# A recurrence and MLP kernel: A of odd chunks stored with exchanged blocks, two K/B buffers, earlier V and r loads

## The chip, the cores and the metric

The kernel runs on one core of one Trainium2 chip. The metric is the device time of one execution in microseconds. A profile is one execution taken by the hardware profiler.

## The reference

For each of 4 batches and 8 heads a 40 x 40 state runs over 768 tokens; its outputs, heads side by side, go through a token-mixing and a channel-mixing MLP:

```
for t in range(S):                                   # S = 768
    y[t]  = r[t] @ state
    Sa    = state @ a[t]
    state = state * w[t][None, :] - outer(Sa, b[t]) + outer(v[t], k[t])
u   = x + (relu(x.T @ w_tok1) @ w_tok2).T            # x: 768 x 320, w_tok1: 768 x 256
out = u + relu(u @ w_ch1) @ w_ch2                    # w_ch1: 320 x 1536
```

All inputs are fp32 (the MLP weights arrive as wide numbers and are split into pairs that TensorE multiplies).

## The kernel before

**Chunks.** Tokens are cut into chunks of 64, 48 in all, numbered g over the batches, 12 per batch. Inside a chunk the recurrence is solved in closed form: a product of A with K and B (px), a triangular 64 x 64 inverse per head, and products with it (ph). From chunk to chunk only the state is handed on (pq, pS, pU); y comes two chunks at a time into the bank yb.

**Preparation** (`t_prep`, one batch in four quarters of 16 tokens): loads w, a, k, b (`pin`, 96 partitions = head x chunk), scans the decays, scales, and stores K/B, A and the decays to the DRAM tiles `sKB`, `sA`, `sP`.

**Pairs** (`t_ab`, `t_a`): two chunks share the buffer `KBp`, loaded from `sKB`, and one of six `AT` buffers, loaded from `sA`. TensorE transposes them (pk, pa) and multiplies (px); the 32 x 32 diagonal blocks go into `Dg`, the blocks off the diagonal into `N21`.

**Solve** (`t_solve`): for a set of eight chunks at once VectorE transposes `Dg` (L748), inverts all 32 x 32 blocks row by row (L770, L772) and transposes the result (L826, L831). In the first two sets it inverts 16 x 16 blocks, and `merge` completes them with TensorE products pm (L927), in four 32 x 32 places of the array.

**Joining the blocks** (`t_b`, per pair): the 64-inverse is made of two 32-inverses T1, T2 and the block T1 N21 T2. With the heads of a chunk in two halves of the partitions, pe = N21 T is computed (L976), copied by ScalarE (`ET`, L984), multiplied again, pt (L1005), and copied into `TBD` (L1011) beside the copies of the diagonal blocks (L968 to L970). ph (L1029) uses `TBD` and `AT`.

**V and r** (`t_load`, `t_v`): v and r of a chunk go into one of three buffers `W2s`, K/B of the chunk into `KB`; pv transposes them (L271, the helper for all transposes).

**MLP** (`t_mlp`): lines L1502 and L1612, the weights of which (`t_piece`: conversion in pieces cv_t, cv_c, stores to sT, sG) are loaded by GpSimd's queue.

**What sets the order.** All work stands in generators; `Planner` runs them in a model of the chip and issues every instruction where its model first finds its engine free, by rank (the numbers of the table `K`). So the order on each engine is fixed when the kernel is built: engines and the SP queue, which issues nearly all DMAs, work in that order and wait by semaphores. When the model sees TensorE idle it puts in a filler (L372), a bf16 product whose result isn't used.

Of the kernel before, what the change touches and what calls it, by code (L numbers as in the profile page):

```python
# [24 lines left out]

K = dict(lat=[200.0, 150.0, 145.0, 90.0], aff=0.92, sets=[8, 8, 8, 8, 8, 8], atn=6, kbp=1, ld=6.75, v=0.89, vg="PA",
         tbd_early=39.4, tbd=[["PD", "AD", "PD", "A"], ["PD", "PD", "A", "P"]], alt_c=1, slack=-10000.0, evm=9.95,
         slack_c=560.87, p_rc=[0, 0, 0, 2], p_a=[0, 2, 0, 1], p_k=[2, 2, 2, 1], solve=[5.59, 4.52, 4.55, 6.79, 6.26,
         -5.24], solve_span=4.19, atomic=0, a=10.07, a_span=3.08, b=2.06, chain=-0.25, evac=0.43, y=-0.77, utr=5.3,
         pem=2, mrg=3.17, ea=9.74, prp=12, psp=12, w=3, c=2, m=2, warm=37, fill=19, fill_cols=4661, prep=[-15.76,  # L30
         -9.38, 9.96, 18.64], prep_step=[2.75, 1.08, 1.04, 1.23], mlp=[11.72, 24.75, 34.32, 41.84], mlp_span=[15.13,
         11.98, 12.78, 11.38], conv_t=6.5, conv_t_span=-10.1, conv_c=3.53, conv_c_span=11.08, conv_after=1)

# [212 lines left out]
def tile_kernel(ctx, tc, r, k, v, w, a, b, wt1, wt2, wc1, wc2, out, dbg=None):  # L246
# [152 lines left out]
    def t_prep(bi):  # L399
# [9 lines left out]
        for q in range(NQ):  # L409
# [18 lines left out]
            def comp(q=q, d=d, ring=ring, tsl=tsl):  # L428
# [518 lines left out]
    def t_b(g):  # L947
# [24 lines left out]

        def pe(z, p, h):
            def f():
                q0, q1 = h * 64, h * 64 + 32
                nc.tensor.matmul(d["pe"][q0:q0 + L, z * NP + p, :], lhsT=o[z]["n21"][q1:q1 + L, p, :],  # L976
                                 rhs=TBt[q1:q1 + L, :, (ci + z) * NP + p], start=True, stop=True)
            return ("PE", (57, 35, "D"), f)

        def etc(h):  # L980
            def f():
                if h == 0:
                    d["et"] = ph.tile([128, 2 * NP, L], F32, tag="ET", name=f"ET{g}", bufs=1)
                nc.scalar.copy(out=d["et"][h * 64:h * 64 + L], in_=d["pe"][h * 64:h * 64 + L])  # L984
            return ("ACT", 372, f)
# [13 lines left out]
        now = yield [etc(0), etc(1)]
        P.rel(tk, now)  # L1000

        def pt(z, p, h):
            def f():
                q0 = h * 64
                nc.tensor.matmul(d["pt"][q0:q0 + L, z * NP + p, :], lhsT=TBn[q0:q0 + L, :, (ci + z) * NP + p],  # L1005
                                 rhs=d["et"][q0:q0 + L, z * NP + p, :], start=True, stop=True)
            return ("PE", (57, 35, "D"), f)

        def tin(h):
            q0 = h * 64  # L1010
            return ("ACT", 372, lambda: nc.scalar.copy(out=TBDb[q0:q0 + L, :, L:2 * L], in_=d["pt"][q0:q0 + L]))  # L1011
        d["pt"], tk = yield from bank("w", [128, 2 * NP, L], f"pt{g}")
        now = yield [pt(*x) for x in zph]
# [808 lines left out]
```

## Time and profile before

| | |
|---|---|
| median of 3 runs | 954.62 us (947.91 to 956.86) |
| the profiled execution | 954.88 us, span 953.2 us |
| TensorE busy | 843.6 us (89%), mean granted clock 0.916 |
| VectorE, ScalarE, GpSimd busy | 607.1 (64%), 531.0 (56%), 227.0 us (24%) |
| DMA | 145.83 MB, mean 153 GB/s |

The span runs from the first to the last instruction; the time adds what lies around it. Matmuls are pipelined, so a busy TensorE is not one at its peak. A wait is put down to what ended it.

### The profile page before, as it was taken

The numbers are of one execution on the slowest core, as the hardware profiler recorded it, in microseconds if no ns is written. First come the engines' busy times: TensorE is split into PE (matmuls) and PEld (weight loads), VectorE is DVE, ScalarE is ACT, GpSimd is POOL, SyncE is SP. The second block draws the span as 40 slices with busy tenths as digits, with TensorE's granted clock in tenths as the row PEclk, the third lists the DMA queues.
The fourth block names the chain that finished last, engine by engine and source line by source line (L and its number), as shares of the span: only waits on it lengthen the run. The fifth ranks groups of instructions, "written<-read, shape, count | busy, mean of one in ns | idle before, by whom it ended". The sixth has DMA issues, their size and how long they took to land.

```text
span 953.2 us, 34564 instructions
## 1 busy us (share of the span) xinstructions
PE 843.6 (89%) x14605; PEld 758.2 (80%) x14605; DVE 607.1 (64%) x1538; ACT 531.0 (56%) x1412; POOL 227.0 (24%) x304
## 2 busy tenths in 40 slices
PE   2666778998898878899998999999989999999997
PEld 2655667887787767788887887999878899998997
DVE  7656885688548978349974498535984544454443
ACT  4266645876659766566675754566535454443221
POOL 5213474343335424021422011001211111001000
PEclk7788886997779869989999998999999999999999
DMA  6698866588585793929458665535356534345522
GB/s 189 177 210 212 202 181 177 144 214 184 154 205 141 180 271 89 233 41 231 132 115 201 147 182 130 110 74 138 82 153 177 127 100 90 74 133 155 183 91 86
DMA packets 244720, 145.83 MB, mean 153 GB/s; under 512 B 205520, under 2 KB 222672, under 8 KB 241488
## 3 DMA queue, kind: packets, MB, share of 16 engines
q1 hardware_dynamic: 238224, 96.37, 44.6%
q0 software_dynamic: 6336, 47.19, 15.4%
q8 instruction: 117, 1.92, 0.9%
q14 instruction: 43, 0.35, 0.1%
HBM read 109.12 MB, written 34.41 MB: 151 GB/s over the span
## 4 chain that ended last, share of the span: by engine, by line
PE 59%; DMA 14%; DVE 12%; issue 6%; ACT 6%; SPq 3%; POOL 0%; DVEq 0%; ACTq 0%; POOLq 0%
PE m L1502 15%; PE m L1612 13%; DMA W2s<-in_r_dram 4%; PE pm L927 3%; SPq L388 3%; PE pq L1095 2%; PE pq L1120 2%; PE pt L1005 2%; PE pv L271 2%; PE ph L1029 2%; DMA cv_t<-in_moe_w_tok_dram 2%; PE yb L372 2%; PE px L670 2%; PE pq L1115 2%; PE pe L976 2%
## 5 line engine op out<-in xcount | busy, mean ns | idle before, releaser
L1612 PE MATMUL m<-ut,wg_c 128*128 128x256 f32 x1152 | 175.5, 294 | 0.2
L1612 PEld LDWEIGHTS m<-ut,wg_c 128*128 128x128 f32 x1152 | 150.0, 191 | 6.6 <-issue 0.9
L1502 PE MATMUL m<-wg_c,hd 128*128 128x320 f32 x864 | 153.6, 321 | 1.3 <-DVE hd L1624 1.1
L1502 PEld LDWEIGHTS m<-wg_c,hd 128*128 128x128 f32 x864 | 130.0, 191 | 5.9 <-DVE hd L1624 1.5
L1622 ACT ACTIVATE hd<-m 128x256 fp32r<-128x256 f32 x144 | 55.3, 384 | 121.3 <-PE m L1612 119.8
L1624 DVE SCALAR_TENSOR_TENSOR hd<-m,hd 128x256 fp32r<-128x256 f32 x144 | 60.8, 422 | 77.3 <-ACT hd L1622 76.4
L1652 DVE TENSOR_TENSOR x<-m,x 128x320 f32<-128x320 f32 x96 | 46.9, 489 | 63.8 <-PE m L1502 63.4
L372 PE MATMUL yb<-ident 128*128 128x192 bf16 x693 | 80.7, 274 | 3.8 <-DVE P L1267 2.0
L385 POOL TENSOR_TENSOR cv_c<-cv_c 128x320 f32<-128x320 f32 (+3 forms) x54 | 58.3, 1086 | 97.8 <-ACT cv_c L1338 70.7
L372 PEld LDWEIGHTS <-ident 128*128 128x128 bf16 x693 | 66.1, 109 | 10.0 <-issue 4.0
L707 ACT ACTIVATE Dg<-px 128x128 f32<-128x128 f32 x144 | 56.1, 390 | 14.0 <-PE px L670 9.7
L1437 POOL DMA_DIRECT2D wg_c<-sG x32 | 17.6, 551 | 149.0 <-PE m L1612 73.7
L271 PE MATMUL pv<-ident,W2s 128*104 128x128 f32 x192 | 32.9, 289 | 19.5 <-DMA W2s<-in_r_dram 16.9
L970 POOL COPY TBD<-TBt 32x256 f32<-32x256 f32 x33 | 22.2, 673 | 111.2 <-PE ph L1029 85.8
L1235 PE MATMUL yb<-KB,RM 128*64 128x40 f32 x768 | 48.0, 230 | 0.0
L385 POOL TENSOR_TENSOR pin<-pin,RC 96x640 f32<-96x640 f32 x19 | 33.8, 1787 | 59.4 <-DVE RC L493 38.1
L1237 PE MATMUL yb<-VSs,RBs 104*64 104x40 f32 x768 | 47.6, 229 | 0.0
L1209 ACT COPY VSs<-pU 40x160 f32<-40x160 f32 x88 | 25.1, 285 | 38.1 <-PE pU L271 36.6
L271 PE MATMUL pk<-ident,KBp 128*104 128x128 f32 x192 | 35.2, 301 | 12.3 <-DMA KBp<-sKB 12.3
L1129 POOL TENSOR_TENSOR RM<-G,upp 64x128 f32<-64x128 f32 x30 | 16.4, 554 | 119.4 <-ACT G L1110 119.1
L641 ACT COPY KBT<-pk 104x512 f32<-104x512 f32 x48 | 27.9, 586 | 26.7 <-PE pk L271 26.1
L1235 PEld LDWEIGHTS yb<-KB,RM 128*64 128x64 f32 x768 | 40.8, 137 | 1.7 <-issue 0.8
(202 smaller groups left out, 1961.8 us busy)
## 6 DMA issues: line engine op xcount, KB each, us to landing
wg_c<-sG POOLq DMA_DIRECT2D x16, 1152.0 KB, 5.9
wg_c<-sG POOLq DMA_DIRECT2D x16, 960.0 KB, 5.5
wg_t<-sT POOLq DMA_DIRECT2D x8, 1280.0 KB, 7.2
sKB<-pin SPq DMA_DIRECT2D x16, 480.0 KB
KBp<-sKB SPq DMA_DIRECT2D x48, 160.0 KB
KB<-sKB SPq DMA_DIRECT2D x48, 160.0 KB
sG<-cv_c SPq DMA_DIRECT2D x24, 192.0 KB
pin<-in_w_dram SPq DMA_DIRECT2D x16, 240.0 KB
```

What stands on the lines that cost most here:

```text
L271: nc.tensor.matmul(out_, lhsT=in_, rhs=idn, start=True, stop=True, is_transpose=True)
L372: nc.tensor.matmul(yb[:, 320:512], lhsT=zf[:, 0:128], rhs=zf[:, 0:192], start=True, stop=True)
L385: return [(e, Port(60 + f * n / 0.96 if e == "DVE" else 140 + 2.24 * n), lambda e=e: engines[e].tensor_tensor(out=out_(), in0=a_(), in1=b_ ...
L388: return ("SP", (ns, data), lambda: nc.sync.dma_start(out=dst(), in_=src()))
L707: return ("ACT", 190 if sl.start == 0 else 392, lambda: nc.scalar.activation(out=Dg[sl, :, ci * NP:(ci + 1) * NP].rearrange("p s n -> p n s"),
L1235: nc.tensor.matmul(dst, lhsT=rms[g - 1 + z][:, h, :], rhs=o["kb"][:, h, :], start=True, stop=False)
L1237: nc.tensor.matmul(dst, lhsT=o["rb"][:, h // 2, q0:q0 + 64], rhs=o["vs"][:, h // 2, 64:DP], start=False, stop=True)
L1502: nc.tensor.matmul(d[key], lhsT=lhs(i, a_), rhs=rhs(i, b_), start=i == 0 and j == 0, stop=i == n - 1 and j == 2)
L1612: nc.tensor.matmul(pt, lhsT=mm_[q][0], rhs=mm_[q][1], start=q == 0, stop=q == len(mm_) - 1)
L1622: nc.scalar.activation(out=hid[key][:, 0], in_=pt, func=AF.Relu)
L1624: now = yield [("DVE", dve(256), lambda: nc.vector.scalar_tensor_tensor(out=hid[key][:, 1], in0=pt, scalar=0.0, in1=hid[key][:, 0].bitcast ...
L1652: now = yield [("DVE", dve(320), lambda: tt(out=x()[:, i], in0=d[("c2", g, i)], in1=x()[:, i], op=ALU.add))]
```

## The change

Seven edits belong together.

- The stores of A go in two halves: even chunks as before, odd chunks with their two 32-row blocks exchanged. Everything that is made of A's rows follows: the mask (`lows`), the copies out of px, the merge's operands and the places in `TBD`, which becomes a view of a slightly longer buffer.
- pe and pt then have, for an even and an odd chunk, inputs and outputs in four different 32 x 32 places; the loop alternates the chunks. The pe bank is half as wide and fully used, so one copy of 128 x 128 takes the place of two of 32 x 256; pt is copied in four pieces, by ScalarE or VectorE.
- `kbp=2`: two K/B buffers.
- `t_load`: the V/r loads wait for the chain of chunk g - 3 alone, not for the batch's preparation or y; the K/B load of the chunk is a step of its own, with its own rank, and waits as before.
- The planner holds an SP issue until it is at most 3.5 us ahead of its DMA model.
- The descriptor area of GpSimd's DMAs in SBUF is 8,192 instead of the default 16,384 bytes per partition.
- The table `K` has new ranks, so the order of all engines is new; it has 521 fillers instead of 693.

```
-K = dict(..., kbp=1, ld=6.75, v=0.89, ..., warm=37, fill=19, fill_cols=4661, ...)
+K = dict(..., kbp=2, ld=6.87, ldk=2.51, back=3500.0, v=1.43, ..., warm=53, fill=33, fill_cols=4527, ...)
...
+                if e == "SP":
+                    t0 = max(t0, self.dma - K["back"])
...
+    lows = [ctile([128, 64], f"low{z}") for z in range(2)]
...
+            for q in range(2):
+                sq = slice(h * 64 + q * 32, h * 64 + q * 32 + 32)
+                nc.gpsimd.affine_select(out=lows[z][sq], in_=lows[z][sq], compare_op=ALU.is_gt, fill=0.0,
+                                        base=32 * (q ^ z), pattern=[[-1, 64]], channel_multiplier=1)
...
-                    dma(lambda: sA[bi].rearrange("c h t e -> h c t e")[:, :, tsl], lambda: A, 580.0, 800.0),
+                    dma(lambda z=z: sA[bi].rearrange("(k z) h t e -> z h k t e", z=2)[z][:, :, slice((q ^ (2 * z)) * QT, (q ^ (2 * z)) * QT + QT)],
+                        lambda z=z: pin[z::2, 1], 440.0, 400.0) for z in range(2)] + [
...
         if g >= 3:
-            yield from chained(g - 3)
-        yield prep_done[bi]
+            for e in range(2):
+                yield chain_done[g - 3][e]
...
-        yield [("SP", (700.0, 960.0), ldkb)]
+        def rest():
+            yield prep_done[bi]
+            if g >= 3:
+                yield from chained(g - 3)
+            yield [("SP", (700.0, 960.0), ldkb)]
+        P.spawn(rest(), g - K["ldk"], now)
...
-        def pe(z, p, h):
-                q0, q1 = h * 64, h * 64 + 32
-                nc.tensor.matmul(d["pe"][q0:q0 + L, z * NP + p, :], lhsT=o[z]["n21"][q1:q1 + L, p, :],
-                                 rhs=TBt[q1:q1 + L, :, (ci + z) * NP + p], start=True, stop=True)
+        def blk(z, h, j):
+            q = 2 * h + (j ^ z)
+            return slice(q * L, q * L + L)
+        def pe(p, h, z):
+                nc.tensor.matmul(d["pe"][blk(z, h, 0), p, :], lhsT=o[z]["n21"][blk(z, h, 1), p, :],
+                                 rhs=TBt[blk(z, h, 1), :, (ci + z) * NP + p], start=True, stop=True)
...
-        now = yield [etc(0), etc(1)]
+        now = yield [("ACT", 290, etc)]
...
-        now = yield [tin(0), tin(1)]
+        now = yield [tin(h, z) for z in range(2) for h in range(2)]
...
-    nc = _bacc.Bacc("TRN2", target_bir_lowering=False, num_devices=1)
+    nc = _bacc.Bacc("TRN2", target_bir_lowering=False, num_devices=1, dynamic_dma_scratch_size=8192)
```

Three places of the new order follow; in each, the first piece is of the kernel before and the second of the change. The first is SP's queue in the first stage, where the loads of the later chunk pairs are issued (`pin1_q`: quarter q of batch 1's w, a, k, b; `KBp`, `AT`: K/B and A of a chunk pair; `W2s`: v and r of a chunk).

```order
L425 DMA pin1_3_578<-in_w_dram 96x640
L425 DMA pin1_3_578<-in_a_dram 96x640
L425 DMA pin1_3_578<-in_k_dram 96x640
L425 DMA pin1_3_578<-in_b_dram 96x640
L388 DMA W2s1_135<-in_v_dram 64x8x40
L388 DMA W2s1_135<-in_r_dram 64x8x40
L388 DMA W2s2_136<-in_v_dram 64x8x40
L388 DMA W2s2_136<-in_r_dram 64x8x40
L388 DMA KBp0_110<-sKB0_156 128x8x40 x2
L388 DMA AT2_114<-sA0_160 128x4x40
```

```order
L434 DMA pin1_1_474<-in_w_dram 96x640
L434 DMA pin1_1_474<-in_a_dram 96x640
L434 DMA pin1_1_474<-in_k_dram 96x640
L434 DMA pin1_1_474<-in_b_dram 96x640
L397 DMA KBp0_119<-sKB0_167 128x8x40 x2
L397 DMA AT2_125<-sA0_171 128x4x40 x2
L434 DMA pin1_2_559<-in_w_dram 96x640
L434 DMA pin1_2_559<-in_a_dram 96x640
L434 DMA pin1_2_559<-in_k_dram 96x640
L434 DMA pin1_2_559<-in_b_dram 96x640
L397 DMA KBp1_120<-sKB0_167 128x8x40 x2
L397 DMA AT3_126<-sA0_171 128x4x40 x2
```

Before, the third pair (`AT2`) stands behind the last loads of batch 1 (`pin1_3`) and two chunks' v and r; now the fourth pair (`AT3`) stands ahead of `pin1_3`, with eight loads of batch 1 between the second pair and it.

The second place is VectorE at the beginning of the first solve (`DT0`: the transposed diagonal blocks, `tmp0_n` and `Tl0`: row n of the inverse, `CP1_3`, `rq1_3`, `RC1_3`: the last quarter of batch 1's preparation, `cv_t`: pieces of an MLP weight).

```order
L493 TENSOR_TENSOR RC1_3_1018<-RC1_3_1018,pin1_3_578 96x2x40 x3
L693 TENSOR_TENSOR AT3_115<-px6_989,low_90 128x4x64
L493 TENSOR_TENSOR RC1_3_1018<-RC1_3_1018,pin1_3_578 96x2x40 x3
L693 TENSOR_TENSOR AT3_115<-px7_990,low_90 128x4x64
L493 TENSOR_TENSOR RC1_3_1018<-RC1_3_1018,pin1_3_578 96x2x40
L748 STREAM_TRANSPOSE DT0_1080<-Dg0_124 128x32x32
L385 TENSOR_TENSOR pin1_3_578<-pin1_3_578 96x640
L770 TENSOR_TENSOR tmp0_1_1125<-Tl0_107,DT0_1080 128x2
L656 COPY ATB8_1127<-pa8_1096 104x512
L772 TENSOR_REDUCE Tl0_107<-tmp0_1_1125 128x2
L1333 TENSOR_SCALAR cv_t2_1_0_1005<-cv_t2_1_0_1005 128x384
L770 TENSOR_TENSOR tmp0_2_1142<-Tl0_107,DT0_1080 128x8
```

```order
L759 STREAM_TRANSPOSE DT0_919<-Dg0_135 128x32x32
L781 TENSOR_TENSOR tmp0_1_939<-Tl0_116,DT0_919 128x2
L467 COPY D1_110<-CP1_2_813 96x40
L473 SCALAR_TENSOR_TENSOR CP1_3_946<-W1_111,D1_110 96x680
L783 TENSOR_REDUCE Tl0_116<-tmp0_1_939 128x2
L666 COPY ATB8_962<-pa8_927 104x512
L487 TENSOR_SCALAR rq1_3_973<-ce1_491 96x80
L506 RECIPROCAL rq1_3_973<-rq1_3_973 96x80
L781 TENSOR_TENSOR tmp0_2_990<-Tl0_116,DT0_919 128x8
L1350 TENSOR_SCALAR cv_t2_1_384_906<-cv_t2_1_384_906 128x384
L500 TENSOR_TENSOR RC1_3_999<-rq1_3_973,CP1_3_946 96x2x40
L783 TENSOR_REDUCE Tl0_116<-tmp0_2_990 128x2x2
```

The last quarter of batch 1's preparation stood ahead of the solve and now stands between its rows, and the first piece of weight that VectorE converts behind the second row is another one (`cv_t2_1_384`).

The third place is TensorE at the first products that join the blocks of pair 20 (`N21_20` of its even, `N21_21` of its odd chunk; `m4` is work of the MLP).

```order
L1612 MATMUL m4_0_0_1_1_6304<-ut_0_5854,wg_0_c1_0_5759 128x256 x8
L976 MATMUL pe20_6300<-TBt2_5713,N21_20_4416 32x32 x8
L976 MATMUL pe20_6300<-TBt2_5713,N21_21_4428 32x32 x8
L1612 MATMUL m4_0_0_1_2_6364<-ut_0_5854,wg_0_c1_0_5759 128x256 x8
L1120 MATMUL pq17_1_6315<-G17_6181,HU16_5956 64x104 x4
```

```order
L1629 MATMUL m4_0_0_2_0_6039<-ut_0_5524,wg_0_c1_0_5440 128x256 x2
L996 MATMUL pe20_6216<-TBt2_5589,N21_20_4295 32x32
L996 MATMUL pe20_6216<-TBt2_5589,N21_21_4335 32x32
L996 MATMUL pe20_6216<-TBt2_5589,N21_20_4295 32x32
L996 MATMUL pe20_6216<-TBt2_5589,N21_21_4335 32x32
L996 MATMUL pe20_6216<-TBt2_5589,N21_20_4295 32x32
L996 MATMUL pe20_6216<-TBt2_5589,N21_21_4335 32x32
L996 MATMUL pe20_6216<-TBt2_5589,N21_20_4295 32x32
```

Eight products of one chunk stood ahead of eight of the other; now a product of the even chunk and one of the odd chunk take turns, up to the sixteenth.

## Rows read from the trace of the kernel before

**Rows 1.** The page's busy times (share of the span, instructions).

```profile
PE 843.6 (89%) x14605; PEld 758.2 (80%) x14605; DVE 607.1 (64%) x1538; ACT 531.0 (56%) x1412; POOL 227.0 (24%) x304
```

**Rows 2.** The table of stretches of the core: from:to and length in us, then busy us (instructions) of PE, PEld, DVE, ACT and POOL, the granted TensorE clock, the DMA share and GB/s.

```profile
0.00:42.00 42.00, 17.64 (x142) 17.25 (x143) 31.95 (x74) 17.12 (x25) 19.30 (x41) 0.72 0.65 182
42.00:130.00 88.00, 58.02 (x670) 52.68 (x670) 59.77 (x152) 51.98 (x107) 30.69 (x23) 0.86 0.90 204
130.00:361.00 231.00, 202.36 (x4964) 172.25 (x4963) 167.58 (x406) 159.41 (x411) 91.30 (x98) 0.82 0.73 183
361.00:862.00 501.00, 480.68 (x8209) 432.71 (x8206) 310.35 (x820) 281.02 (x806) 80.96 (x134) 0.98 0.54 132
862.00:953.00 91.00, 84.94 (x646) 83.32 (x642) 37.50 (x88) 21.45 (x63) 4.76 (x9) 0.98 0.40 131
```

**Rows 3.** The same table for the instructions of line 372 alone (the fillers): busy us of PE and PEld, then clock, DMA share and GB/s.

```profile
130.00:361.00 231.00, 30.75 (x223) 21.86 (x223) 0.82 0.73 183
```

**Rows 4.** The timeline of TensorE in the first stage (start us, us, instruction, and in brackets the idle time before it and what ended it): the K/B transposes of the first and the fourth pair.

```profile
47.13 0.61 PE L271 MATMUL pk<-ident,KBp 128*104 128x128 f32 x4 [1.55 <-DMA KBp<-sKB]
89.18 0.62 PE L271 MATMUL pk<-ident,KBp 128*104 128x128 f32 x4 [0.70 <-DMA KBp<-sKB]
```

**Rows 5.** The timeline of VectorE there: a wait for a weight piece, the solve's first transpose, its second row, and its last transposes.

```profile
80.36 0.36 DVE L1333 TENSOR_SCALAR cv_t<-cv_t 128x384 int32<-128x384 int32 x1 [3.86 <-DMA cv_t<-in_moe_w_tok_dram]
99.80 1.96 DVE L748 STREAM_TRANSPOSE DT<-Dg 128x1024 f32<-128x1024 f32 x1
105.13 0.16 DVE L770 TENSOR_TENSOR tmp<-Tl,DT 128x8 f32<-128x8 f32 x1
127.78 1.96 DVE L826 STREAM_TRANSPOSE TBt<-Tl 128x1024 f32<-128x1024 f32 x1
```

**Rows 6.** The table of stretches again, for 42 to 90 us.

```profile
42.00:66.00 24.00, 15.82 (x193) 14.16 (x190) 9.73 (x24) 10.73 (x20) 3.58 (x2) 0.86 0.98 220
66.00:90.00 24.00, 14.76 (x160) 13.44 (x159) 15.81 (x42) 16.26 (x34) 7.35 (x6) 0.86 0.99 182
```

**Rows 7.** The DMA issues: destination<-source, queue, count, KB of one.

```profile
sKB<-pin SPq DMA_DIRECT2D x16, 480.0 KB
KBp<-sKB SPq DMA_DIRECT2D x48, 160.0 KB
KB<-sKB SPq DMA_DIRECT2D x48, 160.0 KB
pin<-in_w_dram SPq DMA_DIRECT2D x16, 240.0 KB
sA<-pin SPq DMA_DIRECT2D x16, 240.0 KB
sP<-pin SPq DMA_DIRECT2D x16, 240.0 KB
AT<-sA SPq DMA_DIRECT2D x48, 80.0 KB
cv_t<-in_moe_w_tok_dram SPq DMA_DIRECT2D x8, 384.0 KB
```

**Rows 8.** The timeline of TensorE at three places: a run of pm, of pe and of pt, each of 32 instructions.

```profile
133.01 0.68 PE L927 MATMUL pm<-ET,TBn 32*32 32x32 f32 x32 [1.60 <-DVE ET L934]
367.26 1.08 PE L976 MATMUL pe<-TBt,N 32*32 32x32 f32 x32
820.02 1.10 PE L1005 MATMUL pt<-ET,TBn 32*32 32x32 f32 x32
```

**Rows 9.** Groups of instructions by shape (xcount | busy us, mean ns | idle us before, releaser).

```profile
L984 ACT COPY ET<-pe 32x256 f32<-32x256 f32 x48 | 17.4, 362 | 10.1 <-PE pe L976 9.5
L1011 ACT COPY TBD<-pt 32x256 f32<-32x256 f32 x48 | 17.4, 362 | 17.0 <-PE pt L1005 16.6
L699 ACT ACTIVATE N<-px 128x128 f32<-128x128 f32 x38 | 11.9, 313 | 0.0
L1578 ACT CAST ut<-m 64x128 fp32r<-64x128 f32 x24 | 6.2, 260 | 0.0
```

**Rows 10.** The timeline of TensorE behind stage one: the waits for V/r loads.

```profile
218.13 1.21 PE L271 MATMUL pv<-ident,W2s 128*104 128x128 f32 x8 [2.52 <-DMA W2s<-in_r_dram]
342.01 1.07 PE L271 MATMUL pv<-ident,W2s 128*104 128x128 f32 x4 [1.63 <-DMA W2s<-in_r_dram]
346.70 1.06 PE L271 MATMUL pv<-ident,W2s 128*104 128x128 f32 x4 [3.19 <-DMA W2s<-in_r_dram]
394.16 1.07 PE L271 MATMUL pv<-ident,W2s 128*104 128x128 f32 x4 [3.55 <-DMA W2s<-in_r_dram]
514.59 0.62 PE L271 MATMUL pv<-ident,W2s 128*104 128x128 f32 x4 [2.31 <-DMA W2s<-in_r_dram]
```

**Rows 11.** The timeline of SP's queue: the last store of A of batch 0.

```profile
38.25 0.70 SPq L388 DMA_DIRECT2D sA<-pin  x1
```

**Rows 12.** The table of stretches, at a solve.

```profile
288.00:312.00 24.00, 21.01 (x494) 17.67 (x497) 22.54 (x51) 22.51 (x55) 12.81 (x13) 1.00 0.64 162
```

**Rows 13.** The timeline of TensorE: two groups of px, of 32 instructions each.

```profile
331.98 1.10 PE L670 MATMUL px<-KBT,ATB 40*64 40x128 f32 x32 [0.75 <-ACT ATB L658]
351.24 1.98 PE L670 MATMUL px<-KBT,ATB 40*64 40x128 f32 x32
```

More of the change, by code (lines that the diff above doesn't have):

```diff
@@ L23 @@
 LAT = {"PE": 190.0, "ACT": 210.0, "DVE": 130.0, "POOL": 150.0, "SP": 1000.0, "SWD": 1100.0}
[L26 to L32, printed above, removed]
+K = dict(lat=[200.0, 150.0, 145.0, 90.0], aff=0.92, sets=[8, 8, 8, 8, 8, 8], atn=6, kbp=2, ld=6.87, ldk=2.51,
+         back=3500.0, v=1.43, vg="PA", tbd_early=44.18, tbd=[["PD", "AD", "PD", "A"], ["PD", "PD", "A", "P"]],
+         alt_c=1, slack=-20632.66, evm=11.08, slack_c=800, p_rc=[0, 0, 0, 2], p_a=[1, 2, 0, 1], p_k=[0, 2, 2, 0],
+         solve=[5.82, 4.75, 4.78, 3.77, 6.49, -4.01], solve_span=4.09, atomic=0, a=10.15, a_span=4.14, b=2.36,
+         chain=0.38, evac=0.66, y=-0.98, utr=3.21, pem=2, mrg=1.11, ea=9.22, prp=12, psp=12, w=3, c=2, m=2, warm=53,
+         fill=33, fill_cols=4527, prep=[-15.86, -9.43, 9.96, 18.64], prep_step=[2.75, 1.08, 1.04, 2.51], mlp=[11.7,
+         24.73, 34.65, 40.65], mlp_span=[15.08, 11.93, 12.87, 12.38], conv_t=5.75, conv_t_span=-7.0, conv_c=3.53,
+         conv_c_span=11.08, conv_after=1)
 class Port(float):
@@ L290, in tile_kernel @@
         sl = slice(h * 64, h * 64 + 64)
-        nc.gpsimd.memset(low[sl], 1.0)
-        nc.gpsimd.affine_select(out=low[sl], in_=low[sl], compare_op=ALU.is_gt, fill=0.0,
-                                base=0, pattern=[[-1, 64]], channel_multiplier=1)
+        for z in range(2):
+            nc.gpsimd.memset(lows[z][sl], 1.0)
+            for q in range(2):
+                sq = slice(h * 64 + q * 32, h * 64 + q * 32 + 32)
+                nc.gpsimd.affine_select(out=lows[z][sq], in_=lows[z][sq], compare_op=ALU.is_gt, fill=0.0,
+                                        base=32 * (q ^ z), pattern=[[-1, 64]], channel_multiplier=1)
         nc.gpsimd.memset(upp[sl], 1.0)
@@ L692, in e1 @@
         def e1():
-            tt(out=at[:, :, DP + z_ * 64:DP + z_ * 64 + 64], in0=px_[:, :, 0:64], in1=low.unsqueeze(1).to_broadcast([128, NP, 64]), op=ALU.mult)
+            tt(out=at[:, :, DP + z_ * 64:DP + z_ * 64 + 64], in0=px_[:, :, 0:64], in1=lows[z_].unsqueeze(1).to_broadcast([128, NP, 64]), op=ALU.mult)
         def neg(o_, i_):
@@ L705, in e3 @@
         def e3(sl, c0):
-            return ("ACT", 190 if sl.start == 0 else 392, lambda: nc.scalar.activation(
+            return ("ACT", 300 if sl.stop == 128 and sl.start == 0 else 380, lambda: nc.scalar.activation(
                 out=Dg[sl, :, ci * NP:(ci + 1) * NP].rearrange("p s n -> p n s"),
@@ L714, in t_a @@
             yield noff_open
-        e3s = [e3(slice(0, 128), 64), e3(slice(L, 2 * L), 96), e3(slice(3 * L, 4 * L), 96)]
+        b2 = L * (1 - z_)
+        e3s = [e3(slice(0, 128), 64), e3(slice(b2, b2 + L), 96), e3(slice(b2 + 2 * L, b2 + 3 * L), 96)]
         if ea:
@@ L971, in tbd, with etc @@
             return [ops[z] for z in K["tbd"][g >= K["tbd_early"]][q]]
-        def pe(z, p, h):
+        def blk(z, h, j):
+            q = 2 * h + (j ^ z)
+            return slice(q * L, q * L + L)
+        def pe(p, h, z):
             def f():
-                q0, q1 = h * 64, h * 64 + 32
-                nc.tensor.matmul(d["pe"][q0:q0 + L, z * NP + p, :], lhsT=o[z]["n21"][q1:q1 + L, p, :],
-                                 rhs=TBt[q1:q1 + L, :, (ci + z) * NP + p], start=True, stop=True)
[L978 to L985, printed above, removed]
+                nc.tensor.matmul(d["pe"][blk(z, h, 0), p, :], lhsT=o[z]["n21"][blk(z, h, 1), p, :],
+                                 rhs=TBt[blk(z, h, 1), :, (ci + z) * NP + p], start=True, stop=True)
+            return ("PE", (16, 32, "D"), f)
+        def etc():
+            d["et"] = ph.tile([128, NP, L], F32, tag="ET", name=f"ET{g}", bufs=1)
+            nc.scalar.copy(out=d["et"], in_=d["pe"])
         tbd_done = Event()
@@ L995, in t_b, with pt, tin @@
         yield R_et
-        zph = [(z, p, h) for z in range(2) for p in range(NP) for h in range(2)]
-        d["pe"], tk = yield from bank("w", [128, 2 * NP, L], f"pe{g}")
-        yield [pe(*x) for x in zph]
-        now = yield [etc(0), etc(1)]
+        phz = [(p, h, z) for p in range(NP) for h in range(2) for z in range(2)]
+        d["pe"], tk = yield from bank("w", [128, NP, L], f"pe{g}")
+        yield [pe(*x) for x in phz]
+        now = yield [("ACT", 290, etc)]
         P.rel(tk, now)
-        def pt(z, p, h):
+        def pt(p, h, z):
             def f():
[L1004 to L1013, printed above, removed]
+                nc.tensor.matmul(d["pt"][blk(z, h, 0), p, :], lhsT=TBn[blk(z, h, 0), :, (ci + z) * NP + p],
+                                 rhs=d["et"][blk(z, h, 0), p, :], start=True, stop=True)
+            return ("PE", (16, 32, "D"), f)
+        def tin(h, z):
+            sl = blk(z, h, 0)
+            cp = (lambda e: lambda: e(out=TBDb[sl, z * NP:z * NP + NP, L:2 * L], in_=d["pt"][sl]))
+            return [("ACT", 265, cp(nc.scalar.copy)), ("DVE", 250, cp(nc.vector.tensor_copy))]
+        d["pt"], tk = yield from bank("w", [128, NP, L], f"pt{g}")
+        now = yield [pt(*x) for x in phz]
         P.rel(R_et, now)
         yield tbd_done
-        now = yield [tin(0), tin(1)]
+        now = yield [tin(h, z) for z in range(2) for h in range(2)]
         P.rel(tk, now)
```

10 lines of the change are left out of this document (6 added, 4 removed).

## The prediction

> **What bounds the kernel now.** I read the busy shares first: TensorE is busy 89% of the span, and no other engine is near that [rows 1]. A share is a mean over stages, so the second view is the table of five stretches [rows 2]. In 0 to 42 us and 42 to 130 us TensorE is busy for 18 and 58 us, and the DMA engines for 0.65 and 0.90 of the time: a first stage in which TensorE waits for data. In 130 to 361 us (recurrence alone) it is busy for 202 of 231 us, at a mean granted clock of 0.82, so part of that stage ran at 1.2 GHz; 31 of the 202 us are fillers [rows 3]. In 361 to 862 us (recurrence and three MLPs) it is busy for 481 of 501 us at 0.98. The last 91 us are the MLP of batch 3, which needs every token of that batch and so begins when the recurrence is over. The end is therefore the length of stage one, plus TensorE's work in stages two and three with its gaps, plus a constant. Time saved at the front or on TensorE moves the end by as much; time saved on another engine does so only where TensorE waits for it.
>
> The third view is the timeline of the first stage. Chunk pairs 0, 2, 4, 6 must be through before the first triangular solve. K/B data of the first pair is used at 47.13, of the fourth at 89.18 [rows 4]; the solve's transpose begins at 99.80 and the inverse is out from 127.78 [rows 5]. Between 42 and 90 us the DMA share is 0.98 and 0.99, at 220 and 182 GB/s [rows 6]: bytes set this pace, and so does the order in which they are asked for. In the old order all sixteen 240 KB loads of batch 1, six V/r loads, two rounds of batch 1's stores and a weight piece stand ahead of the fourth pair.
>
> **The change, part by part.** The profiled execution took 954.9 us, 0.3 us from the median of 954.62; the sum is made against it.
>
> *Two K/B buffers, new load order (stage one).* A pair is 2 x 160 KB of K/B and 2 x 80 KB of A [rows 7]. In the new order the four pairs have only twelve 240 KB loads between them: 4 x 480 + 12 x 240 = 4,800 KB from 42 us on. At the 201 GB/s of these 48 us (mean of 220 and 182) that is 24 us, so the fourth pair lands near 66 us, not 89. From its use to the solve's transpose the old run needs 99.80 - 89.18 = 10.6 us; the transpose could start at 77. What is late next is a weight piece: right behind the solve's second row VectorE, which works in order, stands at the conversion of cv_t2_1_384, whose load comes another 4 x 240 (batch 1) + 2 x 960 (its stores) + 3 x 160 + 2 x 480 + 2 x 384 = 5,088 KB later, 25 us, so near 92 us. Such a stall is in the old trace too (3.86 us for cv_t) [rows 5]. The old run reaches that row of the solve at 105.13. The gain is then 13 us there, less the last quarter of batch 1's preparation, which now lies inside the solve (seven small products and one large, about 2.5 us). I take **-11 us**. Ends: 0, if the byte queue keeps today's pace, and -20 (99.8 - 77 less 2.5), if the weight piece comes in time.
>
> *Products in four places.* A pair's pe and pt are 32 TensorE instructions each (16 fp32 products, two passes). Today a run of 32 takes 1.08 and 1.10 us [rows 8]; it uses two places of the array. The change alternates an even and an odd chunk, whose blocks lie crosswise, so four places are in use. The nearest row is pm, the same 32x32 products in four places: 32 in 0.68 us [rows 8]. The saving is 0.42 us per run, over 24 pairs and two runs 20 us. Sixteen pairs (32 runs, 13.4 us) fall into stage three, where TensorE is full: all of it counts. Eight pairs (6.7 us) fall into stage two, where real work is (202 - 31) / 231 = 0.74 of the time: 5 us. I take **-18 us**; ends: 0 (the rival below) and -22, if runs at the lower clock gain more.
>
> The Trainium skill, in "TensorEngine Tiling (Array Packing)", section "Restrictions and Gotchas", speaks against this: different row tiles write to different PSUM banks and cannot use one bank at the same time. All four places here write one bank, so by that rule the runs would not overlap and this term would be 0. The pm rows, four row tiles into one bank in 0.68 us, disagree; the rule stays a rival.
>
> *Evacuations.* Of pe: 48 copies of 32x256 at 362 ns become 24 of 128x128; nearest row 313 ns. Of pt: 48 at 362 ns become 96 of 32x128, 49 on ScalarE and 47 on VectorE; nearest row 260 ns for 64x128 [rows 9]. ScalarE: 34.8 us become about 20; VectorE gets some 12 us more. Neither is what TensorE waits for most of the time: 0, with ends of -3 (each pair's path is about 0.5 us shorter) and +13 (a rival).
>
> *V and r loads.* They no longer wait for the outputs y of the chunk three back, only for its state, and are issued singly instead of in couples. The waits of TensorE for these loads after stage one are 2.52, 1.63, 3.19, 3.55 and 2.31 us [rows 10], 13.2 us. The two near 342 us come behind the 960 KB load of MLP 0, which stays; the other three sum to 8.4. I take **-8 us**; ends 0 and -13. Behind an earlier load on SP's queue stand K/B pairs, weight pieces and P loads; all wait less, as the load's own wait ends earlier.
>
> *A stored in halves.* Sixteen stores become 32 of half the size: 16 more issues of 0.70 us on SP [rows 11], hidden except ahead of the first K/B load, where one lies on the path: **+1 us**, ends 0 and +3 (the four of batch 0). Masks, memsets and the merge's operand choice cost a few short instructions in the first 15 us, under the loads of batch 0. The smaller descriptor area for GpSimd's DMAs: 0, since its queue waits for TensorE far longer than for itself. The first V/r loads now come ahead of batch 0's stores, 480 KB in a stretch at a DMA share of 0.65: 0.
>
> Sum: -11 - 18 - 8 + 1 = -36 us, **919 us**.
>
> **The rivals.** *Transfers keep the pace.* For it: the DMA share is already 0.98 and 0.99 there, and the change moves no byte away. Against it: what is moved behind the fourth pair isn't needed before it. Then stage one and the V/r loads give nothing: 954.9 - 18 + 1 = 938.
>
> *The places don't run together.* For it the skill's rule, against it the pm rows: 919 + 18 = 937.
>
> *VectorE becomes the bound.* In 288 to 312 us, at a solve, it is busy for 22.5 of 24 us [rows 12], and the change gives it 12 us more, two copies per pair ahead of a product. If all of this lies on the path: 932. Against it: the planner may give each copy to ScalarE, and most pairs have no solve beside them.
>
> *The clock falls (slower).* Place: the stage from 130 to 361 us. Fewer TensorE microseconds are asked for, and the order has fewer fillers: 203 instead of 246 from the first merge product on, 693 to 521 in all. The engine's time there is part at 1.2 GHz already. Price: one px group takes 1.10 us at the high level and 1.98 at the low one [rows 13], so work goes at 0.56 of the pace. A mean of 0.82 means 36% at the low level: 231 us of stage hold 231 x (0.64 + 0.36 x 0.56) = 194 us of full-clock work. At a mean of 0.65 (70% low) the same work needs 194 / 0.69 = 281 us, +50, and the sum is 919 + 50 = 969. It decides from where +36 eats the gain: 194 / 267 = 0.73 of the pace, 62% low, a mean of about 0.69. Against it: fillers are still put where TensorE would be idle, and the four-place runs squeeze the same columns into less time, as the pm runs do.
>
> That the change isn't there at all is excluded: the order shows the alternating products, both K/B buffers and the moved loads.
>
> **How the numbers follow.** Forecast 0.64, transfers 0.14, places 0.04, VectorE 0.07, clock 0.11. The forecast's own range runs from -20 - 22 - 13 + 1 - 3 = -57 (898) to 0 - 13 + 3 = -10 (945), the -13 being the runs of stage three alone; it takes in 938, 937 and 932. I set 898 to 946, which leaves out the clock and an edge on both sides. A difference of 1% (9.5 us) is about what a measurement of this kernel tells from none. Faster by more than that: 0.61 of the forecast, 0.10 of transfers, 0.04 and 0.07: 0.82. Within 1%: 0.03 + 0.04 + 0.02 of the clock: 0.09. Slower: 0.09.
>
> **What would show it.** Right: runs of 32 pe or pt in about 0.68 us; the first solve's transpose before 82 us and the inverse near 117; the first MLP row near 342 instead of 361; the recurrence over near 826; W2s waits after stage one under 6 us; a granted clock of 0.8 or more between. Wrong: pe and pt still near 1.1 us; the fourth pair's data not before 80 us; VectorE waits in front of ph or the solve; a clock under 0.69 in stage two. New waits on SP's queue, where every load stands in one line, are what I can least see from here.

## The result and the profile after

The changed kernel took 921.59 us (median of 4; 918.99 to 924.24), the kernel before 951.66 beside it: a ratio of 0.968, interval 0.962 to 0.975. A second sitting gave 916.46 against 949.8, 0.964 (0.959 to 0.968). From the second sitting on, medians are of the fast runs where the runs of a kernel fell into a fast and a slow state. The forecast was 919, a gain of 36 us from the profiled 954.9; against the kernel before beside it the gain was 30 and 33 us. The total came out as predicted; the experiments below show that its terms do not all stand as they were added.

The page's busy times after (before: [rows 1]):

```profile
PE 817.0 (89%) x14465; PEld 733.3 (80%) x14465; DVE 619.7 (67%) x1579; ACT 513.2 (56%) x1390; POOL 217.4 (24%) x318
```

To compare stages, each trace is cut at the same events: first merge product (end of stage one), first MLP product, first product of batch 3's MLP. The table of stretches (columns as in [rows 2]) of the kernel before, then of the changed one:

```profile
0.00:129.90 129.90, 75.56 (x801) 69.83 (x802) 91.62 (x226) 69.11 (x132) 49.99 (x64) 0.82 0.82 197
129.90:361.30 231.40, 202.76 (x4968) 172.53 (x4968) 167.98 (x406) 159.64 (x412) 91.60 (x99) 0.82 0.73 182
361.30:864.90 503.60, 483.28 (x8222) 435.39 (x8221) 310.54 (x821) 280.79 (x805) 80.66 (x133) 0.98 0.54 133
864.90:953.20 88.30, 82.03 (x620) 80.47 (x618) 37.00 (x87) 21.45 (x63) 4.76 (x9) 0.98 0.38 124
```

```profile
0.00:118.30 118.30, 67.78 (x706) 62.66 (x707) 84.91 (x210) 61.97 (x120) 42.47 (x66) 0.93 0.81 194
118.30:343.10 224.80, 190.62 (x4784) 162.18 (x4784) 158.56 (x396) 148.34 (x385) 91.92 (x102) 0.80 0.70 178
343.10:832.10 489.00, 476.85 (x8385) 428.11 (x8384) 340.32 (x891) 285.12 (x836) 78.41 (x142) 0.99 0.58 146
832.10:921.60 89.50, 81.77 (x600) 80.39 (x597) 35.87 (x85) 17.80 (x50) 4.57 (x9) 0.97 0.39 129
```

The changed kernel in the second sitting:

```profile
0.00:118.30 118.30, 68.84 (x705) 63.22 (x706) 84.74 (x210) 61.96 (x120) 42.54 (x66) 0.90 0.81 194
118.30:335.30 217.00, 184.18 (x4784) 156.06 (x4784) 157.76 (x396) 148.83 (x385) 92.44 (x102) 0.82 0.72 183
335.30:825.50 490.20, 475.91 (x8385) 426.48 (x8384) 339.90 (x891) 285.05 (x836) 79.86 (x142) 0.99 0.58 146
825.50:913.60 88.10, 80.27 (x600) 78.89 (x597) 35.94 (x85) 17.81 (x50) 4.59 (x9) 0.98 0.39 130
```

Stage one is 11.6 us shorter, stage two 6.6 (second sitting 14.4), stage three 14.6 (13.4), the tail unchanged within 1.2. Between its two profiles the same kernel differs by 7.8 us in stage two: a difference of a few us in one stage of one profile proves nothing.

Stage one, in the timelines of TensorE (the fourth pair's K/B transposes; [rows 4]) and of VectorE (a scan of batch 1's preparation, the copy of the fourth pair's A, the solve's first transpose, its second row, the weight piece, the last transpose; [rows 5]):

```profile
70.70 0.60 PE L274 MATMUL pk<-ident,KBp 128*104 128x128 f32 x4
```

```profile
76.83 1.57 DVE L473 TENSOR_TENSOR_SCAN CP<-W,D 96x680 f32<-96x680 f32 x1 [0.92 <-ACT W L456]
78.33 0.66 DVE L666 COPY ATB<-pa 104x512 f32<-104x512 f32 x1
85.12 2.02 DVE L759 STREAM_TRANSPOSE DT<-Dg 128x1024 f32<-128x1024 f32 x1
92.69 0.10 DVE L781 TENSOR_TENSOR tmp<-Tl,DT 128x8 f32<-128x8 f32 x1
92.83 0.36 DVE L1350 TENSOR_SCALAR cv_t<-cv_t 128x384 int32<-128x384 int32 x1
116.24 1.90 DVE L837 STREAM_TRANSPOSE TBt<-Tl 128x1024 f32<-128x1024 f32 x1
```

The pair is used 18.5 us earlier, the solve begins 14.7 us earlier, and 11.5 us of that are left at its end: its rows wait in line behind preparation and weights. TensorE did not wait for the fourth pair's K/B (no idle time stands in front of it). What the forecast did not have comes after it: the pair's px starts at 79.14, 8.4 us behind its K/B (5.3 before, 94.52 to 89.18), because VectorE's copy of A stands behind the scan. The stall on the weight piece, forecast near 92 us, did not come: VectorE starts the piece right behind the solve's second row, without idle time.

A new wait stands ahead of the first MLP. From TensorE's waits between 118.3 and 343.1 us (total, times, longest), and VectorE's timeline there:

```profile
PE pS L1200 <- DVE RM L1163: 9.5, 2, 7.9
PE pU L274 <- DVE G L1211: 4.7, 1, 4.7
```

```profile
323.36 0.46 DVE L487 TENSOR_SCALAR rq<-ce 96x80 f32<-96x80 f32 x1 [2.35 <-ACT ce L483]
...
334.84 0.28 DVE L1162 TENSOR_TENSOR RM<-pq,upp 128x128 f32<-128x128 f32 x1
```

RM, which the state's chain needs, stands on VectorE's queue behind the last quarter of batch 2's preparation (rq, RC), the first MLP's sums and rows of the solve; TensorE sits idle 7.9 us for it, and 4.7 us for the next work of the chain (G). The second sitting has 6.6 and 4.7 there. No W2s wait is left behind stage one in the first profile, one of 2.6 us in the second, against 13.2 us in five [rows 10].

The copies of pt and pe by shape ([rows 9]):

```profile
L1027 ACT COPY TBD<-pt 32x128 f32<-32x128 f32 x49 | 12.5, 256 | 17.8 <-PE pt L1021 10.5 <-DVE TBD L1027 6.2 <-PE pq L1137 0.6
L1002 ACT COPY ET<-pe 128x128 f32<-128x128 f32 x24 | 6.4, 268 | 3.4 <-PE pe L996 3.1
L1027 DVE COPY TBD<-pt 32x128 f32<-32x128 f32 x47 | 13.5, 287 | 18.3 <-ACT TBD L1027 10.1 <-PE pt L1021 7.4
```

ScalarE spends 18.9 us on them instead of 34.8, VectorE 13.5.

### The profile page after: what moved, and what is told of

Its sections match the earlier page's. It is cut to its first block, busy times and chain, and to the rows that moved or that the text cites. A ratio compares the mean times of both kernels' runs of the same rounds, so it can differ in the third digit from the quotient of the medians.

```text
span 921.6 us, 34301 instructions
## 1 busy us (share of the span) xinstructions
PE 817.0 (89%) x14465; PEld 733.3 (80%) x14465; DVE 619.7 (67%) x1579; ACT 513.2 (56%) x1390; POOL 217.4 (24%) x318
## 4 chain that ended last, share of the span: by engine, by line
PE 56%; DVE 18%; issue 10%; DMA 7%; ACT 5%; SPq 3%; POOL 1%; DVEq 0%; ACTq 0%; POOLq 0%
PE m L1519 15%; PE m L1629 11%; PE ph L1046 3%; PE pm L944 3%; PE pq L1137 3%; PE pq L1112 2%; PE pq L1132 2%; PE px L680 2%; SPq L397 2%; PE yb L1252 2%; PE pk L274 2%; PE pU L274 2%; PE pv L274 2%; DVE pin L394 2%; PE yb L1254 2%
## 5 line engine op out<-in xcount | busy, mean ns | idle before, releaser
L1629 PE MATMUL m<-ut,wg_c 128*128 128x256 f32 x1152 | 172.6, 292 | 3.0 <-issue 1.5
L394 POOL TENSOR_TENSOR cv_c<-cv_c 128x384 f32<-128x384 f32 (+3 forms) x62 | 61.7, 1007 | 93.8 <-ACT cv_c L1355 59.9
L381 PE MATMUL yb<-ident 128*128 128x192 bf16 x521 | 60.5, 267 | 0.0
L274 PE MATMUL pv<-ident,W2s 128*104 128x128 f32 x192 | 36.4, 309 | 18.8 <-DMA W2s<-in_r_dram 18.7
L1252 PE MATMUL yb<-KB,RM 128*64 128x40 f32 x768 | 51.5, 235 | 1.5 <-issue 1.5
L381 PEld LDWEIGHTS <-ident 128*128 128x128 bf16 x521 | 48.2, 106 | 5.5 <-issue 2.2
L1254 PE MATMUL yb<-VSs,RBs 104*64 104x40 f32 x768 | 51.4, 235 | 1.1 <-issue 1.1
L680 PE MATMUL px<-KBT,ATB 40*64 40x128 f32 x768 | 30.9, 296 | 17.7 <-DVE ATB L666 4.7
L1254 PEld LDWEIGHTS yb<-VSs,RBs 104*64 104x64 f32 x768 | 41.9, 144 | 1.1 <-issue 1.1
L274 PEld LDWEIGHTS pv<-ident,W2s 128*104 128x104 f32 x192 | 23.9, 144 | 21.7 <-issue 19.7
```

Source lines behind the costliest of these rows:

```text
L274: nc.tensor.matmul(out_, lhsT=in_, rhs=idn, start=True, stop=True, is_transpose=True)
L381: nc.tensor.matmul(yb[:, 320:512], lhsT=zf[:, 0:128], rhs=zf[:, 0:192], start=True, stop=True)
L394: return [(e, Port(60 + f * n / 0.96 if e == "DVE" else 140 + 2.24 * n), lambda e=e: engines[e].tensor_tensor(out=out_(), in0=a_(), in1=b_ ...
L680: nc.tensor.matmul(bk[z][0][q * 64:q * 64 + 64, p, :], lhsT=d["atb"][z * 64:z * 64 + D, p, q * 64:q * 64 + 64], rhs=ks[h // 4][z * 64:z * ...
L1252: nc.tensor.matmul(dst, lhsT=rms[g - 1 + z][:, h, :], rhs=o["kb"][:, h, :], start=True, stop=False)
L1254: nc.tensor.matmul(dst, lhsT=o["rb"][:, h // 2, q0:q0 + 64], rhs=o["vs"][:, h // 2, 64:DP], start=False, stop=True)
```

## The experiments

Each is held against the changed kernel's 921.6 and 916.5, and by its ratio to the kernel before, run beside it.

### Products two places at a time, and one

The changed kernel with `phz` reordered; the first run goes chunk by chunk, the second place by place. All else keeps its place.

```
-        phz = [(p, h, z) for p in range(NP) for h in range(2) for z in range(2)]
+        phz = [(p, h, z) for z in range(2) for p in range(NP) for h in range(2)]    # two places
+        phz = [(p, h, z) for z in range(2) for h in range(2) for p in range(NP)]    # one place
```

> The changed kernel with one edit: pe and pt go through all products of the even chunk before those of the odd chunk, as before, so that two places of the array are in use at a time; every other instruction keeps its place on its engine. Theory (four places are what shortens the runs, and TensorE's time is the kernel's time in stage three): a run of 32 takes 1.08 to 1.10 us again instead of 0.64 to 0.66, pe and pt together 57.5 us instead of 33.5, and the time is 18 us above the changed kernel's 921.6, near 940. Rival 1 (the shorter runs come from the places' position, not from taking turns): runs stay near 0.65 us, time within 2 us. Rival 2 (the runs lengthen, but waits and fillers take it up): 57.5 us of pe and pt, time up by 6 us or less.

> The changed kernel with one edit: pe and pt go place by place (all eight pairs of heads of one place, then the next), everything else in the same order. With two places in turn the runs had taken 0.85 to 0.91 us, pe and pt 45.0 us in all instead of 33.5, and the time did not rise. Theory A (TensorE's time in the full stage counts, the 7.7 us of it there were hidden by the scatter of the runs): runs of 1.5 us or more, 48 runs, so some 42 us more of pe and pt, of which two thirds lie in stage three: time up by 20 to 30 us against the changed kernel run beside it. Theory B (the kernel waits for its chain of dependences, and TensorE's longer runs fill gaps): up by less than 8 us.

> The changed kernel once more, unaltered, beside the other three: 919 to 924 us, as before. It is what the next run is held against.

Measured: two places 918.46 us, ratio 0.967 (0.962 to 0.972), no difference; one place 931.50, 0.980 (0.976 to 0.984), 15 us more than the changed kernel beside it and between the two forecasts. The timelines of TensorE, of four places, two and one:

```profile
602.41 0.64 PE L996 MATMUL pe<-TBt,N 32*32 32x32 f32 x32
605.86 0.66 PE L1021 MATMUL pt<-ET,TBn 32*32 32x32 f32 x32
```

```profile
593.83 0.85 PE L996 MATMUL pe<-TBt,N 32*32 32x32 f32 x32
597.50 0.90 PE L1021 MATMUL pt<-ET,TBn 32*32 32x32 f32 x32
```

```profile
604.24 1.29 PE L996 MATMUL pe<-TBt,N 32*32 32x32 f32 x32
608.34 1.40 PE L1021 MATMUL pt<-ET,TBn 32*32 32x32 f32 x32
```

pe and pt are busy for 33.5, 45.0 and 66.7 us in all (57.5 in the kernel before). Stages two and three with one place, then stage three with two:

```profile
120.10:337.50 217.40, 190.80 (x4783) 163.93 (x4783) 157.78 (x396) 148.44 (x384) 91.76 (x102) 0.84 0.72 184
337.50:845.00 507.50, 498.44 (x8386) 449.53 (x8384) 340.50 (x891) 285.47 (x836) 78.65 (x142) 0.99 0.56 141
```

```profile
336.40:829.00 492.60, 482.88 (x8385) 434.71 (x8384) 340.91 (x891) 285.49 (x836) 78.53 (x142) 0.99 0.58 145
```

Against the second sitting, stage three has 22.5 us more of TensorE's work and is 17.3 us longer: the first 5 us go into gaps (idle time falls from 14.3 to 9.1), the rest counts in full. In stage two pe and pt take 11 us more and its length does not change (217.4 and 217.0; 224.8 in the first sitting, so this reading is no finer than some 8 us). With two places stage three has 7.0 us more work and is 2.4 us longer, which is inside the scatter. So theory A holds for stage three, with a slack of some 5 us, and theory B for stage two.

### Four places alone

The kernel before with the halves, the four places and the copies, and the old table; v and r as before.

```
-K = dict(..., kbp=2, ld=6.87, ldk=2.51, back=3500.0, v=1.43, ...)
+K = dict(..., kbp=1, ld=6.75, back=1e9, v=0.89, ...)
```

> One part alone on the kernel before: stores of A in halves, four places, the new copies; the old table (one K/B buffer), the old v and r step, no limit on how far SP issues ahead; the planner makes its order anew. By the prediction's terms (-18 for the products, +1 for the stores): 933 to 936. If the products aren't what shortens the kernel: 945 to 955.

Measured: 932.83 us, 0.981 (0.976 to 0.986): 19 us faster, as the two terms said (-18, +1). The stages:

```profile
0.00:129.00 129.00, 77.16 (x818) 70.97 (x818) 96.61 (x226) 68.05 (x130) 47.80 (x71) 0.83 0.83 203
129.00:347.10 218.10, 190.60 (x4965) 161.19 (x4965) 167.97 (x411) 148.40 (x390) 87.36 (x102) 0.88 0.75 183
347.10:842.50 495.40, 473.98 (x8277) 423.74 (x8272) 323.37 (x856) 271.89 (x802) 86.87 (x143) 0.98 0.56 139
```

Not where they said it, though: 13.3 us come in stage two (5 were forecast) and 8.2 in stage three (13). pe and pt take only 9.0 us less in stage two (20.6 to 11.6), so its 13.3 us can't be the products' time alone; the planner made a new order, the copies are new too, and the granted clock was 0.88 instead of 0.82. Which of these gave the rest is not shown, and it is one profile of each kernel.

### V and r: alone, held back, and late

Three runs: the new step alone on the kernel before; the old step in the changed kernel; and the changed kernel in its own order, with each chunk's v and r issued only at its K/B load.

```
         if g >= 3:
-            for e in range(2):
-                yield chain_done[g - 3][e]
+            yield from chained(g - 3)
+        yield prep_done[bi]                      # old step in the changed kernel
...
         def ldkb():
+            flush(g)                             # late: v and r held until here
```

> One part alone on the kernel before: v and r wait only for the state of the chunk three back, K/B is a step of its own at the old rank; the rest as before, with the old table. By the prediction's term of -8: near 944. By the run with the old v and r step in the changed kernel (22 us slower than the changed kernel): 925 to 932. If that step only suits the new ranks: 950 or more.

> The changed kernel with the old step for v and r: the planner holds them for the outputs of the chunk three back and for the batch's preparation, and K/B follows directly. Theory of the prediction (V/r loads that are issued late were worth 8 us): TensorE waits for W2s again, 8 to 13 us in all, time near 930. Rival (the waits went because of the new ranks and the faster first stage): W2s waits under 3 us, time 922 to 925.

> The changed kernel in its own order on every engine, but the v and r loads of a chunk are issued only where its K/B load stands (or just ahead of their transposes, if that comes first). It tells the early transfer from the new order. If early issue is what counts: TensorE's waits for W2s come back, 8 to 20 us, time 925 to 940. If the order that the planner made counts (v and r held for y in the planner cost 22 us or more): W2s waits under 5 us, time within 5 us of the changed kernel.

Measured: alone 950.60 us, 1.003 (0.999 to 1.007), nothing, though the W2s waits behind stage one fell from 13.2 to 8.2 us. Its stages one and three:

```profile
0.00:133.90 133.90, 81.20 (x858) 75.24 (x860) 101.64 (x228) 69.35 (x132) 52.98 (x68) 0.87 0.80 197
365.50:861.20 495.70, 480.08 (x8258) 433.28 (x8254) 324.10 (x823) 278.89 (x806) 85.47 (x140) 0.99 0.54 136
```

Stage three is 7.9 us shorter than in the kernel before and stage one 4.0 us longer, so the forecast 8 us may have come there and been lost again in the new order of the front; one profile of each can't settle it.

Old step: 942.86, 0.992 (0.988 to 0.997), 21 to 26 us lost. The W2s waits behind stage one came back at 10.4 us (8 to 13 were forecast), in a profile at 951.5; the time lost is about twice that. Late: 966.31, 1.020 (1.012 to 1.029), 45 to 50 us lost. What TensorE waited for ahead of the tile W2s in that last run, over the whole span (total, times), and its waits behind stage one (total, times, longest):

```profile
  DMA W2s<-in_r_dram: 59.9, 17
```

```profile
PE pv L274 <- DMA W2s<-in_r_dram: 36.3, 15, 7.5
```

The changed kernel has one wait of 18.7 us in stage one too, and 0 to 2.6 us behind it.

So the early loads carry the new order: its transposes pv stand earlier among TensorE's work (`v` 1.43 instead of 0.89), and without the data they stop everything behind them. In the old order the same loads gain nothing in all. The next run closes the square.

### The changed code with the old table

```
-K = dict(..., kbp=2, ld=6.87, ldk=2.51, back=3500.0, v=1.43, ...)
+K = dict(..., kbp=1, ld=6.75, ldk=6.75, back=1e9, v=0.89, ...)
```

> The changed kernel's code with the old table (one K/B buffer, old ranks, no limit on how far SP issues ahead): four places and the new v and r step, without the new ranks. Four places alone gave 933, v and r alone nothing. If v and r are worth 8 us once TensorE has less to do: near 925. If they need the new ranks: 930 to 936. If all the rest of the gain is v and r: 917 to 921.

Measured: 929.91 us, 0.984 (0.977 to 0.990), the same as four places alone. What lies between this and the changed kernel, 8 to 13 us by the times and 15 to 19 by the ratios, needs the new table and the new v and r step together: the table without the step is slower than either (943). Which entries of the table do it (ranks, or the limit on how far SP issues ahead) was not tried.

### One K/B buffer, and a control

```
-kbp=2
+kbp=1
```

```
-lat=[200.0, 150.0, 145.0, 90.0]
+lat=[198.0, 150.0, 145.0, 90.0]
```

> The changed kernel with one K/B pair buffer instead of two; the planner makes its order anew. Theory of the prediction (the second buffer lets the first four pairs through early): the first solve's transpose slips from 85 to about 97 us, the inverse from 116 to about 127, time near 932. Rival (it is the order of batch 1's loads behind the pairs that does it, a single buffer would be enough): transpose before 89 us, time 922 to 926.

> A control: the changed kernel, with the latency that the planner's model gives a TensorE product lowered from 200 to 198 ns. No buffer, wait or amount of work changes, only the order in places. It tells how much of a difference an order alone makes when nothing is gained or lost. If the order is a matter of small tuning: within 3 us of 921.6. If the order chosen by the table is a lucky one: 5 to 15 us slower.

Measured: one buffer 917.54 us, 0.964 (0.958 to 0.971); control 921.01, 0.967 (0.960 to 0.973). Neither differs from the changed kernel, and the forecast 932 for one buffer did not come. With one buffer:

```profile
0.00:126.40 126.40, 73.27 (x759) 67.17 (x760) 92.30 (x225) 66.95 (x128) 48.73 (x73) 0.91 0.82 201
126.40:361.50 235.10, 200.92 (x5018) 168.82 (x5018) 167.77 (x419) 154.57 (x411) 91.23 (x104) 0.80 0.70 177
361.50:828.60 467.10, 459.83 (x8144) 413.51 (x8139) 322.55 (x858) 274.49 (x803) 72.06 (x131) 1.00 0.57 144
```

Stage one did become 8 us longer, as the theory had it, and the tail still starts at 828.6, between the changed kernel's 825.5 and 832.1. The order is another one, so this alone doesn't say that stage one is worth nothing.

### Stage one delayed, order kept

```
+                if g == 4 and z == 0:
+                    for i in range(10):
+                        nc.sync.dma_start(out=junk[i], in_=lanes(w, 3)[:, 0:QT])
                 nc.sync.dma_start(out=kbp[:, :, z, 0:D], ...)
```

> The changed kernel in its own order, with ten transfers of 240 KB (rows of w of batch 3, from DRAM to DRAM, read by nobody) put on SP's queue ahead of the third chunk pair's K/B. 2.4 MB at the 200 GB/s of that stretch delay the third and fourth pair by about 12 us; nothing else is changed. Theory of the prediction (the end moves as much as the first stage): the first solve's transpose near 97 us instead of 85, the inverse near 128, time 10 to 13 us above the changed kernel's 916 to 922, near 930. Rival (with one K/B buffer the transpose came 9 us later and the end did not move, so later stages take the delay up): the same delay of the solve, time up by less than 5 us.

Measured: 920.47 us (918.68 to 928.71), 0.976 (0.968 to 0.984).

```profile
0.00:126.20 126.20, 70.70 (x702) 64.53 (x702) 84.58 (x210) 62.05 (x120) 42.49 (x66) 0.86 0.81 201
126.20:340.60 214.40, 179.83 (x4784) 152.80 (x4784) 158.54 (x396) 148.50 (x384) 92.40 (x102) 0.85 0.74 187
340.60:827.50 486.90, 475.30 (x8385) 426.50 (x8384) 340.14 (x891) 285.15 (x836) 78.69 (x142) 0.99 0.58 147
```

The transfers delayed stage one by 7.9 us, less than the 12 meant. By the medians the end moved by -1 to 4 us, by the ratios (0.976 to 0.964 and 0.968) by 8 to 12, and the intervals overlap. Against the profile of the second sitting 7.9 us at the first merge product are 5.3 at the first MLP and 2.0 at the tail, with profiles of one kernel that differ by as much. Whether a late first stage is made up later stays open.

### Without fillers

```
     def filler():
+        return
         nc.tensor.matmul(yb[:, 320:512], ...)
```

The 521 fillers are left out; their results were never used.

> The changed kernel in its own order with its 521 fillers left out; every other instruction stays. The rival of the falling clock: the granted clock of the stage between the first merge product and the first MLP, 0.80 to 0.82 now, falls to 0.69 or less, and the time rises by 20 to 50 us. Against it (the real products hold the clock by themselves, the fillers only fill): 0.78 or more, time within 5 us of the changed kernel.

Measured: 919.05 us, 0.971 (0.964 to 0.978): by the medians -3 to 3 us, by the ratios 3 to 7, with intervals that overlap, so no difference that these runs can tell. The profile is of the slowest of its four runs (926.11).

```profile
119.10:342.30 223.20, 176.18 (x4609) 151.03 (x4609) 158.96 (x396) 148.22 (x385) 92.62 (x102) 0.72 0.70 179
```

The mean granted clock of stage two fell from 0.80 and 0.82 to 0.72, and the real products took 176.2 us instead of 168.5 and 161.5 (busy time less fillers of 22.1 and 22.7). The stage is as long as before (223.2; 224.8 and 217.0): its idle time and the fillers' had been slack, as far as the 7.8 us between those two profiles let one see.

## Why the prediction came out

**The total was right** (919; 921.6 and 916.5), in part by luck, as the terms below show. So were most of its marks: inverse at 116.2 (near 117), first MLP at 343.1 (342), last products of the recurrence at 822.6 and 816.0 (826), pe and pt runs of 0.64 to 0.66 us (0.68), W2s waits of 0 to 2.6 us (under 6), clock 0.80 and 0.82 (0.8 or more). The solve's transpose came at 85.1, not before 82: the fourth pair was used at 70.7 (66 was the forecast for its landing), and 14.4 us passed from there to the transpose, not 10.6.

**Four places, -18:** the size is shown by the run with them alone (-19 with the stores). The step "eight pairs fall into stage two: 5 us" failed as reasoning: TensorE's time there costs nothing in the changed order (one place, no fillers), and "TensorE is full: all of it counts" holds in stage three beyond some 5 us of gaps. The traces' 14.4 us less of pe and pt there (37.0 to 22.5) would by that be worth 9 to 10, an estimate. So the products' own time explains about half of the 19 us; that the term came out whole is luck, and what gave the other half stays open. The rule weighed there, from the Trainium skill, "TensorEngine Tiling (Array Packing)", "Restrictions and Gotchas", that row tiles can't use one PSUM bank at once, does not show: 32 instructions of four row tiles into one bank take 0.64 us, of one tile after the other 1.29.

**V and r loads, -8:** the step that failed is adding up old waits as a term of its own. Alone the edit gains nothing in all. In the changed kernel its absence costs 21 to 26 us, or 45 to 50 with the order kept, for W2s waits of 10.4 and 36.3 us. It is the condition of the new table; the two together gave 8 to 13 us (15 to 19 by the ratios), where this term and stage one's had been put at 19.

**Stage one, -11:** the front did come 11.6 us earlier, but not on the forecast path. The transpose was put at 77 us, with a stall on the weight piece up to 92; it came 8 us later (4.7 of them because the pair was used later, 3.1 up to its px, behind the late copy of its A), and the stall did not come. The two errors cancel: the solve's second row came at 92.7. That the size is right is in good part luck. That the end moves with the front is not shown: one buffer gave 8 us of it back at no cost in an order of its own, and the delay with the order kept moved the end by something between -1 and 12 us.

**Evacuations, 0; halves, +1:** copies came out as costed (18.9 us on ScalarE, 13.5 on VectorE). They weren't tried by themselves, nor were the limit on SP's issues and the smaller descriptor area.

**Rivals.** VectorE does become a wait, 12.6 us ahead of the first MLP, but by its order there (RM behind other work), not by the new copies. The clock rival fell: its price let TensorE's slower work stretch the stage, +26 us at a mean of 0.72 by its own formula, and what 0.72 cost lies within the scatter (-3 to 7 us). It also priced all work by px (1.10 and 1.98 us [rows 13]); a run of pe in the changed kernel takes 0.66 us at a granted clock of 0.50 (at 139.50 and 249.67 us) and 0.63 at 1.00 (at 188.21). That transfers keep their pace is excluded by the fourth pair's use at 70.7.

No run beats the changed kernel clearly; one K/B buffer is as fast.

## What to carry to other kernels

Waits in an old trace are not prices that can be added: here an edit that only makes data come earlier gained nothing until the order used it, and an order that used it lost more than those waits when it came late. Before a saving on the busiest engine is counted in a stage, look at what fills its gaps: a stage with 34 us of idle time and 22 us of fillers did not visibly feel 11 us of extra products or a clock of 0.72. Test an edit both ways, alone on the old kernel and undone in the new one; where the two disagree, as 0 and 21 to 26 us here, the parts depend on each other.

## What the runs showed of the hardware

A run of 32 instructions (16 products of 32x32 in two passes) took 0.64 to 0.66 us in four places in turn and 1.28 to 1.42 in one after another. With two places in turn it took 1.08 to 1.10 where both chunks used the same two [rows 8], but 0.85 to 0.91 where the second chunk used the other two: at the change of chunk 20 instructions reach into one stretch of 0.1 us, against at most 12 in the kernel before. Such a run in four places hardly depends on the granted clock: pe took 0.66 us at 0.50 and 0.63 at 1.00, while a group of px took 1.98 and 1.10 [rows 13]. Fillers did raise the granted clock of stage two, from 0.72 to 0.80 and 0.82, without a gain in time that the runs can tell.
